# Two edits to the start of a fused attention and FFN kernel: the second weight's maxima in other PSUM banks, and the first weight's parts traced with every third attention slot

## The chip, the cores and the metric

The kernel runs on one core of one Trainium2 chip. The metric is the device time in microseconds of one execution; times of runs are given as the median of several. A profile is one execution with the hardware profiler on. Engines are PE (TensorE), DVE (VectorE), ACT (ScalarE), POOL (GpSimd) and SP (SyncE, which here issues most transfers).

## The reference, cut to what matters

```python
def _attn_ref(q, k, v, s):                      # B=8, H=8, S=576, D=64, float32
    scores = np.matmul(q, k.transpose(0, 1, 3, 2)) / sqrt(D)
    cum = np.cumsum(np.maximum(s, 0.0), axis=-1)
    bias = -(cum[:, :, :, None] - cum[:, :, None, :])
    scores = np.where(causal, -1e9, scores + np.minimum(bias, 0.0))
    attn = exp(scores - max); attn = attn / (sum(attn) + 1e-9)
    return np.matmul(attn, v)

def _moe_ref(x, w_in, w_out):                   # x is 4608 x 512, d_ff = 2048
    h = x @ w_in
    g = np.where(h >= 1, h, np.where(h <= -1, 0.0, (h + 1) ** 2 / 4))
    return g @ w_out
```

The attention output, with its heads laid side by side, is the x of the FFN. `w_in` and `w_out` arrive as 64-bit floats, which the kernel takes as pairs of 32-bit integers.

## The kernel before, in words

**Attention.** A job is a pair of heads and a part of the query rows (`hf` 0: 320 rows, `hf` 1: 256 rows). There are 64 jobs; each batch has eight, four with `hf` 0 and then four with `hf` 1. Jobs 0 to 3 are thus the first part of batch 0 and jobs 4 to 7 its second part. A job has eight slots (`att_slot(j, k)`): slot 0 prepares operands, slots 2 to 7 compute six units of scores (`scores`, matmuls at L432 for the jobs with float32 operands, L435 and L436 for the others), slot 7 also computes the output of the job before (`att_out`, L524 or L535). A unit of scores goes from PE to DVE (L441, masks and takes the minimum), ACT (L452, exponential), DVE (L466 or L494, the scale) and POOL and ACT, and is transposed on PE (jobs 0 to 3) or by a DMA. `x_split` (L552, L553) turns an output into the FFN's x in two float16 halves.

**Weights.** Each weight comes in 16 parts of 128 x 512. `load(c)` issues the transfer on SP (L199). `decode(c)` makes float32 out of the 64-bit pattern: ACT L207, DVE L208 and L209, and then either ACT L214 and DVE L215, or DVE L217 and L218. A scale is found from the parts' maxima, and `split(c)` makes two float16 halves (ACT L256, then POOL L259 and L262 or DVE L264; the second weight also has ACT L261). For the first weight, `row_scale` finds a scale for each four parts, and `row_shares` (L245 on) joins the four scales. For the second, `scale(g)` (L225 to L234) finds one for each eight parts: `column_max` transposes a column of maxima to a row on PE (L111, tile row_wo) and DVE takes the maximum (L113); `spread` multiplies it by ones on PE (L121, tile col_wo), and DVE copies the column out (L122).

**PSUM.** There are eight banks: pool `ps_s` has two (tag s), for score tiles, the outputs at L535, and all row and col tiles; `ps_h` has two, for h and the transposes of jobs 0 to 3; `ps_y` has four (y0 to y3), for the outputs of jobs 0 to 3, which stay there until their x is made, and then for the sums of the second FFN layer.

**FFN.** The FFN works in blocks (batch, `hf`) of 16 tiles: `ffn_h` computes h (L594) with ACT L606, DVE L609 and L610, ACT L620 and POOL L621 behind it; `ffn_y` multiplies with the second weight (L633). In the first block all 16 h come first, then y0 and y1, then y2 and y3.

**The order.** The kernel is traced in a program order. A planner then orders each engine's instructions by a priority, the traced position, and gives buffers out as they come free; `tc.high_priority(offset=n)` puts a block n positions further ahead. The score minimum at L441 has a lead of 10000; the FFN's element work, the x tiles and the second weight's tasks one of 6000.

At the start, the trace puts the loads of three parts of the first weight first, and then the 32 slots of jobs 0 to 3. With every second slot goes one part of the first weight (L678 to L692): decode part c, load part c + 3, split part c - 4, and after each fourth part `row_scale`. Then come `row_shares` and the last four splits under a lead (L695 to L701), the x tiles of jobs 0 to 3, and six tasks of `w2_tasks` (L664 to L676): eight decodes, `scale(0)`, eight splits, and the same for group 1. The main loop (L710 on) traces one or two attention slots, two more tasks of the second weight, and a step of the FFN each time round. The second weight's first three loads wait for `w1.r[1]`, the scale of parts 4 to 7.

Of the kernel before, what the change touches and what calls it, by code (L numbers as in the profile page):

```python
# [9 lines left out]
F32 = mybir.dt.float32  # L10
# [12 lines left out]
P = 128  # L23
NPAIR = H // 2
NKT = DM // P
# [10 lines left out]
LEAST_A = 2.0 ** -5  # L36
# [29 lines left out]
OUT_K = 7  # L66
W2_RATE = 2
W2_FIRST = 6
FIRST_N = 1
CH_N = 2  # L70

# [6 lines left out]
def attention_ffn(ctx: ExitStack, tc: tile.TileContext, qT, kT, vn, s, w_in, w_out, yT):  # L78
# [8 lines left out]
    ps_s = ctx.enter_context(tc.tile_pool(name="ps_s", bufs=2, space=PSUM))  # L87
    ps_h = ctx.enter_context(tc.tile_pool(name="ps_h", bufs=2, space=PSUM))
    ps_y = ctx.enter_context(tc.tile_pool(name="ps_y", bufs=1, space=PSUM))
# [5 lines left out]
    def pow2floor(out, in_, least):  # L95
        V.tensor_scalar(out, in_, least, None, ALU.max)
        V.tensor_scalar(out.bitcast(I32), out.bitcast(I32), 0x7F800000, None, ALU.bitwise_and)
# [7 lines left out]
    ones = cp.tile([P, P], BF16, name="ones")  # L105
    G.memset(ones, 1.0)

    def column_max(src, name):

        row = ps_s.tile([P, 512], F32, tag="s", name=f"row_{name}")  # L110
        T.transpose(row[:1, :P], src, ident)  # L111
        top = ap.tile([P, 1], F32, tag="top", name=f"top_{name}")
        V.tensor_reduce(top[:1], row[:1, :P], axis=AX, op=ALU.max)  # L113
        return top[:1]

    def spread(dst, top, name):

        t16 = ap.tile([P, 1], BF16, tag="t16", name=f"t16_{name}")
        V.tensor_copy(t16[:1], top)
        col = ps_s.tile([P, 512], F32, tag="s", name=f"col_{name}")  # L120
        T.matmul(col[:, :1], ones[:1], t16[:1], start=True, stop=True)  # L121
        V.tensor_copy(dst, col[:, :1])  # L122

# [44 lines left out]
    NW = 16  # L168
# [7 lines left out]
    class Weights:  # L176
# [48 lines left out]
        def scale(self, g, least):  # L225
            bound, r = self.bound[g], self.r[g]
            t = cp.tile([P, 1], F32, name=f"t_{self.name}{g}")
            V.tensor_reduce(t, self.peak[:, g * self.size:(g + 1) * self.size], axis=AX, op=ALU.max)
            top = column_max(t, f"{self.name}{g}")
            self.exponent(top)  # L230
            V.tensor_scalar(top, top, least, None, ALU.max)
            spread(bound, top, f"{self.name}{g}")
            V.reciprocal(r, bound)
            V.tensor_scalar(r, r, 2.0 ** 14, None, ALU.mult)  # L234

# [30 lines left out]
    w1 = Weights(  # L266
        "wi", lambda c: w_in[c // 4 * P:(c // 4 + 1) * P, c % 4 * NC:(c % 4 + 1) * NC, :],
        WO, WI, ((gp, "g", G_BUFS),), 1, by_rows=True,
    )
# [10 lines left out]
    def load_v(b):  # L280
        for p in range(NPAIR):
            v = vraw[b, p] = ap.tile([P, NB, P], F32, tag="vraw", bufs=4, name=f"v{b}_{p}")
            G.memset(v[TAIL:, NB - 1], 0.0)
            nc.sync.dma_start(v[:, :NB - 1], vn[b, p, :SP - P].rearrange("(j p) n -> p j n", p=P))
            nc.sync.dma_start(v[:TAIL, NB - 1], vn[b, p, SP - P:])

    def batch_start(b):
        c = ap.tile([P, NPAIR], F32, tag="csc", name=f"c{b}")
        for p in range(NPAIR):
            v = vraw[b, p].rearrange("p j n -> p (j n)")  # L290
            V.tensor_reduce(c[:, p:p + 1], v, axis=AX, op=ALU.max, apply_absolute_value=True)
        t = ap.tile([P, 1], F32, tag="mt", name=f"mt{b}")
        V.tensor_reduce(t, c, axis=AX, op=ALU.max)
        top = column_max(t, f"m{b}")
        pow2floor(top, top, TINY)
        m = msc[b] = ap.tile([P, 1], F32, tag="mb", name=f"mb{b}")
        spread(m, top, f"m{b}")
        r = rcs[b] = ap.tile([P, 1], F32, tag="rcs", name=f"rc{b}")
        V.reciprocal(r, m)
        V.tensor_scalar(r, r, 4096.0, None, ALU.mult)  # L300
# [41 lines left out]
    def plain(n, hf):  # L342
        return jobs.index((n, hf)) < PLAIN_JOBS
# [4 lines left out]
    def att_load(n, hf):  # L348
# [4 lines left out]
        if whole(n, hf):  # L353
            for t, src, c0 in zip(operands(n, hf), (qT, kT), (q0, 0)):
                sv = src[b, h0:h0 + 2, :, c0:W].rearrange("h d n -> d h n")
                (FIRSTQ if jobs.index((n, hf)) < FIRST_N else LOADQ).dma_start(t[:D, :, :W - c0], sv)
            return
        rq = ap.tile([P, 2, N], F32, tag="rq", bufs=1, name=f"rq{n}_{hf}")
        rk = ap.tile([P, 2, W], F32, tag="rk", bufs=1, name=f"rk{n}_{hf}")
        for t, src, c0 in ((rq, qT, q0), (rk, kT, 0)):  # L360
            sv = src[b, h0:h0 + 2, :, c0:W].rearrange("h d n -> d h n")
            for d0 in (0, D):
                (FIRSTQ if jobs.index((n, hf)) < FIRST_N else LOADQ).dma_start(t[d0:d0 + D], sv)
        raws[n, hf] = rq, rk

    def att_prep(n, hf):

        q0, N, _ = HALF[hf]
        W = q0 + N
        cd = cumd[2 * n:2 * n + 2].rearrange("h l n -> l h n")  # L370
        if not whole(n, hf) and not split_tiles:
            split_tiles.extend(operand_tiles(F32R, "s"))
            constant_rows(*split_tiles[1])
        Qc, Kc = operands(n, hf) if whole(n, hf) else split_tiles[1]
        if jobs.index((n, hf)) < CH_N:
            for hd in range(2):
                r = ch[2 * n + hd:2 * n + hd + 1]
                CUMQ.dma_start(Qc[D:D + 2, hd, :N].bitcast(F32), r[:, :, q0:W].bitcast(F32))
                CUMQ.dma_start(Kc[D + 2:D + 4, hd, :W].bitcast(F32), r[:, :, :W].bitcast(F32))
        else:  # L380
            CUMQ.dma_start(Qc[D:D + 2, :, :N].bitcast(F32), cd[:, :, q0:W])
            CUMQ.dma_start(Kc[D + 2:D + 4, :, :W].bitcast(F32), cd[:, :, :W])
        if whole(n, hf):
            return
        rq, rk = raws.pop((n, hf))
        (Q1, K1), (Q2, K2) = split_tiles
        A.copy(Q1[:, :, :N], rq)
        A.copy(K1[:, :, :W], rk)  # L388
        A.copy(Q2[:D, :, :N], rq[:D])
        V.tensor_tensor(Q1[D:, :, :N], rq[D:], Q1[D:, :, :N].bitcast(F32), ALU.subtract)  # L390
        V.tensor_tensor(K2[:D, :, :W], rk[:D], K1[:D, :, :W].bitcast(F32), ALU.subtract)  # L391

    def v_prep(n):

        b, p = n // NPAIR, n % NPAIR
        v, r = vraw.pop((b, p)), rcs[b]
        VT = vts[n] = ap.tile([P, 2, NB, P], F16, tag="vt", bufs=5, name=f"vt{n}")
        G.tensor_scalar(VT[:, 0], v, r, 1.0, ALU.mult, ALU.mult)
        if n < V_POOL:
            G.tensor_scalar(v, v, r, 1.0, ALU.mult, ALU.mult)  # L400
            G.tensor_tensor(VT[:, 1], v, VT[:, 0], ALU.subtract)
        vbs[n] = VT, v, r

    def v_low(n):
        VT, v, r = vbs.pop(n)
        if n >= V_POOL:
            with tc.issue_after(ttr[0]):
                V.scalar_tensor_tensor(VT[:, 1], v, r, VT[:, 0], ALU.mult, ALU.subtract)
# [148 lines left out]
    def att_slot(j, k):  # L557

        if j < len(jobs):
            n, hf = jobs[j]  # L560
            if k == 0:
                att_prep(n, hf)
            if plain(n, 0):
                if k in (1, 4) and hf == 1 and j < PLAIN_JOBS + 2:
                    v_prep(2 * (j - PLAIN_JOBS) + k // 4)
            elif hf == 0 and k == 1:
                v_prep(n)
            elif hf == 0 and k == V_K:
                v_low(n)
            if k >= 2:  # L570
                scores(n, *UNITS[hf][k - 2])
            if k == 3 and j + 1 < len(jobs):
                att_load(*jobs[j + 1])
            if k == 1 and j % (2 * NPAIR) == V_J + (j < 2 * NPAIR) and j // (2 * NPAIR) + 1 < B:
                load_v(j // (2 * NPAIR) + 1)
            if k == 5 and j + 1 < len(jobs) and jobs[j + 1][0] % NPAIR == 0 and jobs[j + 1][1] == 0:
                with tc.issue_after(ttr[0]):
                    batch_start(jobs[j + 1][0] // NPAIR)
        if k == OUT_K and 1 <= j <= len(jobs) and j != NPAIR:
            while j == len(jobs) and late:  # L580
                late.pop(0)()
            att_out(*jobs[j - 1])
# [92 lines left out]
                w2.split(c)  # L675
                yield  # L676

    for j in range(NPAIR):  # L678
        for k in range(8):
            if k % 2 == 0:  # L680
                c = 4 * j + k // 2
                w1.decode(c)
                w1.load(c + 3)
                if c >= NKT:
                    w1.split(c - NKT)
                if c % NKT == NKT - 1:
                    w1.row_scale(c // NKT, LEAST_A)
            if (j, k) == (0, 2):
                load_v(0)
            if (j, k) == (0, 6):  # L690
                batch_start(0)
            att_slot(j, k)  # L692
    while late:
        late.pop(0)()
    with tc.high_priority(offset=SCALE_LEAD):  # L695
# [9 lines left out]
    tasks = w2_tasks()  # L705
    for _ in range(W2_FIRST):
        next(tasks)

    t = 8 * NPAIR
# [56 lines left out]
```

## Time and profile before

| what | value |
| --- | --- |
| median of 3 runs | 1100.36 us (1099.31 to 1100.73) |
| the profiled execution | 1098.98 us |
| its span | 1097.2 us |
| mean granted TensorE clock | 0.984 of full speed |
| DVE busy | 79% |
| ACT busy | 66% |
| POOL busy | 60% |

The span is the time from the first to the last instruction of the profiled execution; about 1.8 us lie around it. A row of the timeline has the start and the length in us, the engine, the line of the kernel, the operation, the tile written and the tiles read, the shape and a count; in brackets stands how long the engine had been idle before, and what ended that. Rows of one line that follow each other are merged into one.

### The profile page before, as it was taken

Reading aid. Unit: us, or ns where it says so; the run is one execution under the profiler, and the core shown is the slowest. Engines: PE = TensorE matmul, PEld = TensorE weight load, DVE = VectorE, ACT = ScalarE, POOL = GpSimd, SP = SyncE. Lnnn points to the kernel's source line nnn. Section 1 sums busy time; section 2 is a strip of 40 time slices with the busy share of each in tenths; the row PEclk is TensorE's granted clock in tenths of the full one; section 3 lists DMA queues with packets and bytes.
Section 4 is the critical chain, followed back from the end, with each engine's and each line's share of the span. In section 5 each row is a group of like instructions: output and inputs, shape, how many; then the busy total and the mean of one; then the engine's idle time right before and its main releaser. Section 6 shows DMA issues by size and latency. Waiting matters only on the chain. (4 is left out here: it accounts for less than half of the span.)

```text
span 1097.2 us, 25029 instructions
## 1 busy us (share of the span) xinstructions
PE 1014.7 (92%) x8494; PEld 779.6 (71%) x8494; DVE 862.9 (79%) x2379; ACT 722.7 (66%) x1707; POOL 657.8 (60%) x1139
## 2 busy tenths in 40 slices
PE   1567898999999999999999999899999999999998
PEld 0334566687778877787778877787777877887787
DVE  7998986678788878788788778787888888887533
ACT  4867683567567765877577765776577765777432
POOL 2843486666567656666567665666566666765522
PEclk9998999799999999999999999999999999999999
DMA  8835245546357763777366753766276753677300
GB/s 241 240 119 172 77 101 112 124 107 167 92 116 164 133 145 87 161 143 151 88 146 144 160 124 84 160 134 166 71 161 131 154 127 73 153 137 139 68 25 20
DMA packets 300839, 140.33 MB, mean 128 GB/s; under 512 B 237608, under 2 KB 286632, under 8 KB 300712
## 3 DMA queue, kind: packets, MB, share of 16 engines
q1 hardware_dynamic: 291008, 128.80, 52.2%
q10 hardware_dynamic: 9704, 9.93, 3.2%
q8 instruction: 67, 1.10, 0.4%
q14 instruction: 60, 0.49, 0.1%
HBM read 71.00 MB, written 9.73 MB: 74 GB/s over the span
## 5 line engine op out<-in xcount | busy, mean ns | idle before, releaser
L594 PE MATMUL h<-x,WI 128*128 128x256 f16 (+1 forms) x3072 | 461.4, 290 | 11.9 <-DVE u L610 7.8
L633 PE MATMUL y<-g,WO 128*128 128x256 f16 (+1 forms) x3072 | 446.2, 287 | 1.9 <-ACT g L620 1.9
L594 PEld LDWEIGHTS <-WI 128*128 128x128 f16 x3072 | 287.9, 99 | 105.0 <-issue 22.1
L633 PEld LDWEIGHTS <-WO 128*128 128x128 f16 x3072 | 288.0, 98 | 85.4 <-issue 5.7
L621 POOL TENSOR_TENSOR g<-u,g 128x320 f16<-128x320 f32 (+1 forms) x256 | 207.0, 808 | 172.0 <-ACT g L620 164.0
L452 ACT ACTIVATE p<-p,mn 64x64 f32<-64x64 f32 (+4 forms) x320 | 179.4, 561 | 118.3 <-DVE mn L441 84.6
L606 ACT ACTIVATE u<-h,ub,us 128x320 f32<-128x320 f32 (+1 forms) x256 | 149.3, 583 | 131.8 <-PE h L594 130.0
L609 DVE SCALAR_TENSOR_TENSOR h<-h,ws,u 128x320 f32<-128x320 f32 (+1 forms) x256 | 132.8, 519 | 87.7 <-ACT u L606 84.1
L499 POOL TENSOR_SCALAR pb<-p,rs 128x256 f16<-128x256 f32 (+4 forms) x148 | 94.1, 636 | 142.1 <-DVE rs L495 88.7
L502 POOL TENSOR_TENSOR pb<-p,pb 128x256 f16<-128x256 f32 (+4 forms) x148 | 156.0, 1054 | 9.8
L441 DVE CUSTOM_DVE_ANT_0 p<-s,mask 64x64 f32<-64x64 f32 (+4 forms) x320 | 134.8, 422 | 34.2 <-PE s L436 21.6
L505 DVE SCALAR_TENSOR_TENSOR pb<-p,rs,pb 128x256 f16<-128x256 f32 (+4 forms) x148 | 127.8, 864 | 22.3 <-POOL pb L499 21.7
L610 DVE SCALAR_TENSOR_TENSOR u<-u,r,h 128x320 f32<-128x320 f32 (+1 forms) x256 | 130.5, 510 | 7.4
L435 PE MATMUL s<-K1s,Q1s 128*128 128x288 f32 (+4 forms) x312 | 118.1, 379 | 10.1 <-DVE Q1s L390 5.0
L500 ACT ACTIVATE p<-p,rs 128x192 f32<-128x192 f32 (+4 forms) x148 | 84.2, 569 | 51.5 <-DVE rs L495 49.2
L620 ACT CAST g<-u 128x320 f16<-128x320 f32 (+1 forms) x256 | 108.1, 422 | 6.5 <-DVE u L610 6.3
L501 POOL TENSOR_SCALAR pb<-p 128x256 f16<-128x256 f32 (+4 forms) x148 | 87.6, 592 | 16.7 <-ACT p L500 12.6
L436 PE MATMUL s<-K2s,Q2s 68*128 68x288 f32 (+4 forms) x312 | 96.2, 308 | 0.1
L535 PEld LDWEIGHTS <-vt 128*64 128x64 f16 x1464 | 68.5, 112 | 19.9 <-issue 14.0
L535 PE MATMUL px<-pt,vt 128*64 128x256 f16 (+3 forms) x1464 | 77.2, 257 | 2.7 <-DMA pt<-pb 2.6
L435 PEld LDWEIGHTS s<-K1s,Q1s 128*128 128x128 f32 (+1 forms) x312 | 56.7, 182 | 19.5 <-PE s L436 4.5
L391 DVE TENSOR_TENSOR K2s<-rk,K1s 64x1152 fp32r<-64x1152 f32 (+1 forms) x52 | 62.9, 1209 | 5.9 <-ACT K1s L388 5.1
(134 smaller groups left out, 1034.8 us busy)
## 6 DMA issues: line engine op xcount, KB each, us to landing
rk<-in_k_dram SPq DMA_DIRECT2D x56, 288.0 KB
wir<-in_moe_w_in_dram SPq DMA_DIRECT2D x16, 512.0 KB
v<-in_v_dram SPq DMA_DIRECT2D x32, 256.0 KB
wor<-in_moe_w_out_dram SPq DMA_DIRECT2D x16, 512.0 KB
rk<-in_k_dram SPq DMA_DIRECT2D x48, 160.0 KB
rq<-in_q_dram SPq DMA_DIRECT2D x48, 160.0 KB
rq<-in_q_dram SPq DMA_DIRECT2D x56, 128.0 KB
out_dram<-o ACTq DMA_DIRECT2D x32, 160.0 KB
```

Source lines behind the costliest of these rows:

```text
L435: T.matmul(sc[:R, :c1 - c0], Q1[:, hd, qo:qo + R], K1[:, hd, c0:c1], start=True, stop=False)
L441: ttr[0] = V.tensor_tensor_reduce(out=Pt[:R, c0:c1], in0=sc[:R, :c1 - c0], in1=mask[:R, mo:mo + c1 - c0], scale=-0.125, scalar=3.0e38 if m ...
L452: A.activation(Pt[:R, :W], Pt[:R, :W], AF.Exp, bias=m2[:R], scale=-1.0, accum_out=sums[n, i][:R, hd:hd + 1])
L502: G.tensor_tensor(los[1], pw, his[1], ALU.subtract)
L505: V.scalar_tensor_tensor(los[0], pv, rs[:R, :1], his[0], ALU.mult, ALU.subtract)
L535: T.matmul(px[hd * D:(hd + 1) * D, lo:N], vts[n][:, vl, j, hd * D:(hd + 1) * D], PT[:, 4 * j + 2 * hd + pl, lo:], start=(m == 0), stop=(m ...
L594: T.matmul(h[:, :N], WI[4 * kt + ft // 4][:, wl, ft % 4 * P:(ft % 4 + 1) * P], x[:, kt, xl], start=(n == 0), stop=(n == 3 * NKT - 1),)
L606: first = A.activation(u, h[:, :N], AF.Relu, bias=ubi[b], scale=usc[b]).ins
L609: V.scalar_tensor_tensor(h[:, :N], h[:, :N], wsc[b], u, ALU.mult, ALU.max)
L610: V.scalar_tensor_tensor(u, u, r, h[:, :N], ALU.min, ALU.mult)
L621: G.tensor_tensor(g[:, 1], u, g[:, 0], ALU.subtract)
L633: T.matmul(ys[b, hf, m][:, :N], WO[8 * (m // 2) + ft // 2][:, wl, c0:c0 + P], g[:, gl], start=(ft == 0 and n == 0), stop=(ft == NFT - 1 an ...
```

## The change

`column_max` and `spread` get a parameter `bank`, the pool and the tag of their tile. `scale`, which only the second weight uses, passes y2 for the row tile and y3 for the col tile. The calls of `batch_start` and `row_shares` stay with the two banks of `ps_s`.

The loop over the 32 slots of jobs 0 to 3 now traces a part of the first weight with every third slot, which makes 11 parts (0 to 10); parts 11 to 15 follow behind the last slot. What a part does is the same.

```diff
+W1_SLOTS = 3
...
-    def column_max(src, name):
+    def column_max(src, name, bank=(ps_s, "s")):
-        row = ps_s.tile([P, 512], F32, tag="s", name=f"row_{name}")
+        row = bank[0].tile([P, 512], F32, tag=bank[1], name=f"row_{name}")
...
-    def spread(dst, top, name):
+    def spread(dst, top, name, bank=(ps_s, "s")):
...
-        col = ps_s.tile([P, 512], F32, tag="s", name=f"col_{name}")
+        col = bank[0].tile([P, 512], F32, tag=bank[1], name=f"col_{name}")
...
-            top = column_max(t, f"{self.name}{g}")
+            top = column_max(t, f"{self.name}{g}", (ps_y, "y2"))
...
-            spread(bound, top, f"{self.name}{g}")
+            spread(bound, top, f"{self.name}{g}", (ps_y, "y3"))
...
-    for j in range(NPAIR):
-        for k in range(8):
-            if k % 2 == 0:
-                c = 4 * j + k // 2
-                w1.decode(c)
-                w1.load(c + 3)
-                if c >= NKT:
-                    w1.split(c - NKT)
-                if c % NKT == NKT - 1:
-                    w1.row_scale(c // NKT, LEAST_A)
-            if (j, k) == (0, 2):
-                load_v(0)
-            if (j, k) == (0, 6):
-                batch_start(0)
-            att_slot(j, k)
+    def w1_task(c):
+        w1.decode(c)
+        w1.load(c + 3)
+        if c >= NKT:
+            w1.split(c - NKT)
+        if c % NKT == NKT - 1:
+            w1.row_scale(c // NKT, LEAST_A)
+
+    c = 0
+    for t in range(8 * NPAIR):
+        if t % W1_SLOTS == 0:
+            w1_task(c)
+            c += 1
+        if t == 2:
+            load_v(0)
+        if t == 6:
+            batch_start(0)
+        att_slot(t // 8, t % 8)
+    for c in range(c, NW):
+        w1_task(c)
```

## The prediction

> **What bounds the kernel now.** I read the page first, for the engines over the whole span.
>
> ```profile
> span 1097.2 us, 25029 instructions
> PE 1014.7 (92%) x8494; PEld 779.6 (71%) x8494; DVE 862.9 (79%) x2379; ACT 722.7 (66%) x1707; POOL 657.8 (60%) x1139
> ...
> PE   1567898999999999999999999899999999999998
> ```
>
> TensorE is the bound, 92% busy, and what it lacks lies in the first slices. Neither edit touches a matmul of the FFN or of the attention, so the sum is about TensorE's lost time near the start: when it stood still, and when it ran at a low granted clock. Next came the table of stretches, whose columns are: stretch, length, busy PE, PEld, DVE, ACT, POOL (with counts), PE clock, DMA share, GB/s.
>
> ```profile
> 27.40:97.50 70.10, 46.02 (x146) 24.47 (x145) 65.14 (x202) 52.18 (x121) 39.15 (x58) 1.00 0.63 180
> 97.50:128.00 30.50, 22.25 (x120) 13.58 (x119) 26.83 (x64) 20.21 (x33) 9.30 (x11) 0.83 0.32 105
> 128.00:165.00 37.00, 35.97 (x251) 24.43 (x250) 32.98 (x78) 30.87 (x62) 29.95 (x38) 1.00 0.44 98
> 165.00:180.00 15.00, 15.00 (x118) 10.48 (x117) 8.41 (x24) 6.81 (x16) 9.87 (x15) 1.00 0.66 125
> 180.00:192.00 12.00, 8.17 (x64) 6.20 (x62) 9.57 (x43) 3.81 (x11) 6.76 (x9) 0.83 0.38 100
> 192.00:200.00 8.00, 6.88 (x41) 4.08 (x42) 5.10 (x17) 4.20 (x14) 5.79 (x15) 0.50 0.58 136
> 200.00:209.00 9.00, 9.00 (x37) 5.93 (x36) 6.25 (x21) 5.08 (x15) 5.23 (x16) 0.54 0.68 154
> 209.00:1097.20 888.20, 867.47 (x7717) 688.29 (x7716) 688.96 (x1879) 587.74 (x1418) 543.93 (x957) 1.00 0.56 122
> ```
>
> Up to 165 us VectorE is the bound (65.14 of 70.10, 26.83 of 30.50, 32.98 of 37.00). From 209 us TensorE is (867.47 of 888.20). Between them, from 180 to 209, TensorE loses time though VectorE has room: it stands still 12.00 - 8.17 + 8.00 - 6.88 = 4.95 us, and the clock costs it up to 12 x 0.17 + 8 x 0.50 + 9 x 0.46 = 10.2 us more, 15.1 us together. The timeline of TensorE and of the x tiles says why.
>
> ```profile
> 180.04 1.47 PE L594 MATMUL h<-x,WI 128*128 128x256 f16 x12
> ...
> 198.51 0.47 ACT L552 ACTIVATE x<-px,shares_wi 128x256 f16<-128x256 f32 x1 [0.30 <-PE px L535]
> ```
>
> The first FFN block has run out by 180.04, and the second can't go on: it wants the attention outputs of jobs 6 and 7 (batch 0, second half), and the last of them becomes x at 198.51. Attention jobs 4 to 7 are what ends last, so what the change does is read from when they run.
>
> **The bank edit.** The maxima of the second weight pass through a row tile and a col tile for each of two groups. Now they take banks of pool ps_s, two banks that the score tiles use too; afterwards they take y2 and y3.
>
> ```profile
> 85.95 0.47 DVE L441 CUSTOM_DVE_ANT_0 p<-s,mask 128x320 f32<-128x320 f32 x1
> ...
> 65.97 0.64 SPq L356 DMA_DIRECT2D K1w<-in_k_dram  x1
> ...
> 104.34 5.88 PE L594 MATMUL h<-x,WI 128*128 128x320 f16 x24 [3.53 <-DVE u L610]
> ...
> 117.25 0.27 PE L111 MATMUL row_wo<-ident,t_wo 128*1 128x128 f32 x1
> ...
> 121.60 0.17 PE L121 MATMUL col_wo<-t_wo,ones 1*128 1x1 bf16 x1
> 121.70 1.02 PE L432 MATMUL s<-K1w,Q1w 68*128 68x448 f32 x2
> ...
> 136.13 0.92 PE L432 MATMUL s<-K2w,Q2w 68*128 68x448 f32 x2
> ...
> 138.65 0.27 PE L111 MATMUL row_wo<-ident,t_wo 128*1 128x128 f32 x1
> ...
> 144.33 0.16 PE L121 MATMUL col_wo<-t_wo,ones 1*128 1x1 bf16 x1 [0.53 <-DVE t_wo L119]
> 144.41 0.75 PE L432 MATMUL s<-K2w,Q2w 68*128 68x288 f32 x2
> ```
>
> Both groups show one pattern. The last scores of job 3 are read at 85.95, and job 4's key operand is asked for at 65.97, yet its first score stands directly behind col_wo, at 121.70, with TensorE idle 3.53 us ahead of 104.34. At the second group no score is issued from 137.05 (136.13 + 0.92) to 144.41, 7.36 us, and again the next stands directly behind col_wo. My reading: the maxima are traced under a lead of 6000, ahead of the scores, so their tiles take their turn at the two banks first, and the scores queue behind a maximum that still waits for eight decoded parts. With banks of their own the scores owe them nothing. Bounds for what this moves job 4: nothing at the low end, 121.70 - 104.34 = 17.4 us at the high end, the first place where TensorE had nothing else; at the second group nothing to 7.36 us.
>
> It can't all reach the end, because VectorE is nearly full there: attention pulled forward pushes FFN and decoding work back, except where VectorE was idle. It was idle 30.50 - 26.83 + 37.00 - 32.98 = 7.7 us from 97.5 to 165. I take 7 us for how much earlier the last x of the first batch is ready; 0 and the 15.1 us above are the ends. As TensorE is the bound behind it, that time comes off the end. I count no clock gain in the 7: the gap becomes shorter, but the idleness that lowers the clock need not go.
>
> The new wait costs nothing. y2 and y3 hold outputs of jobs 2 and 3 until they become x behind 97.63 (row below), well ahead of 117.25. The first FFN sums in y2 and y3 need parts 8 to 15 of the second weight, which wait for the second maximum in any case. If that cover were gone, the row would wait, and behind it on TensorE the h tiles: for the longest h wait above, 3.53 us.
>
> On the low clock from 192 to 209: TensorE was busy 6.88 of 8 us and 9 of 9, and it was still granted 0.50 and 0.54. [...]
>
> **The slot edit.** Every part of the first weight moves from slot 2c to slot 3c, and parts 11 to 15 come behind all 32 slots of jobs 0 to 3. One part issues a load on SP, one or two ScalarE passes and these on VectorE (columns: count, busy us, mean ns):
>
> ```profile
> L208 DVE TENSOR_SCALAR_CACHE_REDUCE WO<-WO 128x512 f32<-128x512 f32 x25 | 16.8, 676 | 3.8 <-ACT WO L207 3.8
> L209 DVE TENSOR_SCALAR WO<-WO 128x512 int32<-128x512 int32 x25 | 13.2, 536 | 0.0
> ...
> L217 DVE SCALAR_TENSOR_TENSOR WO<-wir,WO 128x512 int32<-128x512 int32 x8 | 7.5, 940 | 0.0
> L218 DVE SCALAR_TENSOR_TENSOR WO<-wir,WO 128x512 int32<-128x512 int32 x8 | 6.9, 863 | 0.0
> L215 DVE SCALAR_TENSOR_TENSOR WO<-wir,WO 128x512 int32<-128x512 int32 x8 | 5.8, 726 | 0.0
> ```
>
> That is 0.68 + 0.54 + half of (0.94 + 0.86 + 0.73) = 2.5 us a part, so 12.5 us for five parts pass from ahead of the last attention slots to behind them. Which of the two ended last ahead of the FFN?
>
> ```profile
> 87.94 0.29 DVE L698 TENSOR_SCALAR shares<-shares_wi,rc 128x4 f32<-128x4 f32 x1
> 97.63 0.53 ACT L552 ACTIVATE x<-px,shares 128x320 f16<-128x320 f32 x1 [2.37 <-PE px L524]
> ```
>
> The weight's shares are there at 88.23, and the last attention output of jobs 0 to 3 at 97.63, 9.4 us later. So the attention is late and the edit moves the right side forward, by up to 9.4 us; but with 12.5 us moved behind it, the shares end at up to 100.7, 3.1 us later than 97.63. The ends for the first full h are thus 9.4 us earlier and 3.1 us later, nearly even once the shares' chain and the attention meet in the middle. An earlier h alone would only bring the stop at 180 earlier, as long as job 7 isn't earlier too. So I count 0. SP's weight loads stand behind attention loads more often; TensorE waited for no attention operand after the first score tiles, so that is 0 as well. The second weight's first three loads wait for the scales of parts 4 to 7, so they start later too. VectorE fills that with attention; the cost shows only if it idles.
>
> **The sum.** The profiled execution took 1098.98 us (span 1097.2 and 1.8 around it): 1098.98 - 7 + 0 = 1092.0. The median of the runs is 1100.36, 1.4 us more, so I forecast 1100.36 - 7 = 1093.4 us. About 0.2%, 2.2 us, is what a measurement of this kernel can tell from no change.
>
> **The rivals.** *The whole gap goes.* If jobs 4 to 7 keep pace with the first FFN block, the idle time and the low clock from 180 to 209 both go: 1100.36 - 15.1 = 1085.3. For it: job 4 could start 17.4 us earlier. Against it: VectorE had only 7.7 us to spare.
>
> *Nothing moves.* The scores may come late because the planner puts them there and not for the banks, or VectorE's full stretch eats the shift: 1100.4. For it: from 97.5 to 128 VectorE was 88% busy (26.83 of 30.50), and scores not traced with a lead may stay behind the h tiles.
>
> *Slower: the first weight is finished too late.* The last five parts, with their scale and shares, end behind the attention, the second weight's loads start late, and VectorE has nothing ready. The first full h comes 3.1 us later, and the second weight's first maximum slips by up to the raw loads' delay, the 2.5 us of a part. It decides from the point where the shares end later than the last px of job 3; then 3.1 + 2.5 = 5.6 us less what the bank edit returns, about 1 us in that case: 1100.36 + 4.6 = 1105. For it: only 9.4 us of room for 12.5 moved. Against it: VectorE filled some of 27.4 to 97.5 with second-weight work that can wait.
>
> **How the numbers follow.** Forecast 0.46, whole gap 0.14, nothing moves 0.18, first weight late 0.22. Faster is 0.46 + 0.14 = 0.60, within 0.2% 0.18, slower 0.22. The range goes from the whole gap, 1085, to the late weight, 1105, which leaves out about 0.2 for larger swings of either sign. The forecast case alone spans 1088 to 1098.
>
> **What would show it.** Right: the first score of job 4 stands well ahead of 121.70 and no longer behind col_wo; scores are issued between the second row_wo and col_wo; the last x of batch 0's second half comes near 191 instead of 198.51; stretches behind 209 take what they took. The slot edit is right at zero if the first full h stays within 3 us of 97.5. Wrong: job 4's first score still waits until about 120 (the banks weren't it); or it is early and x is not (VectorE took it back); or the clock drops elsewhere; or shares land behind 100.

## The result and the profile after

The changed kernel takes 1095.26 us (median of 15 runs) against 1101.24 us for the kernel before on the same chip (15 runs). The ratio is 0.9943, 95% interval 0.9931 to 0.9954, so it is faster by 0.57%, or 6.3 us. One run of each kernel, 1286.8 and 1198.7 us, was disturbed and is left out of the ratio. The profiled execution took 1094.18 us with a span of 1092.4, 4.8 us less than that of before. The lines shown from here on have numbers one higher than in the kernel before.

The page first: TensorE's busy time is the same within 2 us, and its slices differ only among the first seven (the very first is 1 before and 3 now).

```profile
span 1092.4 us, 25031 instructions
PE 1012.9 (93%) x8494; PEld 779.2 (71%) x8494; DVE 857.4 (78%) x2379; ACT 722.4 (66%) x1707; POOL 659.5 (60%) x1139
...
PE   3657799999999999999999999899999999999998
```

The table of stretches, with the columns of the prediction's:

```profile
27.40:97.50 70.10, 43.59 (x129) 24.36 (x130) 61.91 (x193) 54.10 (x121) 35.34 (x57) 1.00 0.53 165
97.50:128.00 30.50, 23.40 (x136) 13.73 (x135) 29.76 (x81) 18.67 (x35) 16.12 (x21) 0.89 0.77 198
128.00:165.00 37.00, 33.08 (x237) 22.01 (x236) 31.74 (x80) 29.01 (x56) 29.58 (x34) 1.00 0.40 88
165.00:180.00 15.00, 15.00 (x107) 10.65 (x105) 8.79 (x29) 7.03 (x13) 7.53 (x9) 1.00 0.22 58
180.00:192.00 12.00, 9.15 (x82) 6.49 (x80) 7.98 (x33) 6.31 (x19) 8.18 (x18) 0.96 0.44 114
192.00:200.00 8.00, 7.25 (x46) 5.62 (x47) 4.06 (x16) 4.29 (x14) 4.16 (x12) 0.50 0.96 163
200.00:209.00 9.00, 9.00 (x68) 6.60 (x67) 5.58 (x18) 4.68 (x14) 4.00 (x10) 0.74 0.45 111
209.00:1092.40 883.40, 863.68 (x7677) 685.27 (x7675) 686.92 (x1874) 585.86 (x1413) 543.14 (x956) 1.00 0.55 123
```

I work out the loss from 180 to 209 as the prediction did. The idle time is 2.85 + 0.75 = 3.60 us, and the clock costs up to 12 x 0.04 + 8 x 0.50 + 9 x 0.26 = 6.82 us. Together that is 10.4 us, where it was 15.1. The difference of 4.7 us is what the two profiled spans differ by (4.8). Behind 209 us little changed: TensorE lacks 883.40 - 863.68 = 19.7 us there, 20.7 before.

The timeline of TensorE shows where the scores of jobs 4 to 7 went:

```profile
84.23 0.16 PE L122 MATMUL col_wi<-t_wi,ones 1*128 1x1 bf16 x1 [3.12 <-DVE t_wi L120]
84.44 3.33 PE L433 MATMUL s<-K1w,Q1w 68*128 68x448 f32 x4
...
118.48 0.75 PE L433 MATMUL s<-K2w,Q2w 68*128 68x288 f32 x2 [1.85 <-DVE mn L442]
...
126.60 0.27 PE L112 MATMUL row_wo<-ident,t_wo 128*1 128x128 f32 x1
...
135.84 0.17 PE L122 MATMUL col_wo<-t_wo,ones 1*128 1x1 bf16 x1
...
143.26 0.27 PE L112 MATMUL row_wo<-ident,t_wo 128*1 128x128 f32 x1
...
143.64 1.02 PE L433 MATMUL s<-K2w,Q2w 68*128 68x448 f32 x2
...
148.95 0.92 PE L433 MATMUL s<-K2w,Q2w 68*128 68x448 f32 x2
...
152.24 0.17 PE L122 MATMUL col_wo<-t_wo,ones 1*128 1x1 bf16 x1
...
165.94 1.14 PE L433 MATMUL s<-K2w,Q2w 68*128 68x288 f32 x4
...
177.72 0.17 PE L122 MATMUL col_m<-t_m,ones 1*128 1x1 bf16 x1
177.82 0.75 PE L433 MATMUL s<-K2w,Q2w 68*128 68x288 f32 x2
```

Job 4 (K1w) starts at 84.44, not at 121.70, and all its scores and those of job 5 (K2w) are out before the first row_wo. Job 4's first score again stands directly behind a maximum's spread, this time col_wi, the first weight's, which uses the score banks in both kernels; no run moves that one. Scores now also stand between the second row_wo and col_wo; they are job 7's (K2w). But two new stops appear in job 7: no score from 149.87 to 165.94, and none from 167.1 to 177.82, where the next stands directly behind col_m, the spread of the next batch's maximum. The x tiles of the second half of batch 0 show what arrives:

```profile
124.22 0.47 ACT L553 ACTIVATE x<-px,shares_wi 128x256 f16<-128x256 f32 x1 [0.63 <-PE px L536]
145.74 0.46 ACT L553 ACTIVATE x<-px,shares_wi 128x256 f16<-128x256 f32 x1
183.53 0.47 ACT L553 ACTIVATE x<-px,shares_wi 128x256 f16<-128x256 f32 x1 [0.56 <-PE px L536]
195.23 0.47 ACT L553 ACTIVATE x<-px,shares_wi 128x256 f16<-128x256 f32 x1 [1.78 <-PE px L536]
```

Before, these four came at 156.74, 170.51, 187.53 and 198.51. Job 4 is 32.5 us earlier and job 7 only 3.3 us, and the second FFN block needs them all. (In the repetition of the changed kernel, e11 below, job 7's x comes at 197.38, so the 3.3 is 1.1 there.) The experiments ask three things: what each edit is worth alone, whether the banks were the cause, and why 32.5 us become 3.3.

### The profile page after: what moved, and what is told of

Same layout as the page of the kernel before. It is cut to its first block, busy times and chain, and to the rows that moved or that the text cites. A ratio compares the mean times of both kernels' runs of the same rounds, so it can differ in the third digit from the quotient of the medians.

```text
span 1092.4 us, 25031 instructions
## 1 busy us (share of the span) xinstructions
PE 1012.9 (93%) x8494; PEld 779.2 (71%) x8494; DVE 857.4 (78%) x2379; ACT 722.4 (66%) x1707; POOL 659.5 (60%) x1139
## 4 chain that ended last, share of the span: by engine, by line
PE 65%; DVE 10%; ACT 5%; issue 4%; DMA 2%; POOL 2%; ACTq 1%; DVEq 0%; POOLq 0%
PE y L634 27%; PE h L595 26%; PE px L536 4%; PE s L436 3%; PE s L437 3%; DVE pb L506 2%; DVE h L610 2%; DVE p L442 1%; DMA pt<-pb 1%; PE s L433 1%; ACT u L607 1%; DVE K2s L392 1%; DVE Q1s L391 1%; ACT p L453 1%; DVE u L611 1%
## 5 line engine op out<-in xcount | busy, mean ns | idle before, releaser
L442 DVE CUSTOM_DVE_ANT_0 p<-s,mask 64x64 f32<-64x64 f32 (+4 forms) x320 | 135.1, 423 | 34.4 <-PE s L437 20.4
L611 DVE SCALAR_TENSOR_TENSOR u<-u,r,h 128x320 f32<-128x320 f32 (+1 forms) x256 | 130.6, 510 | 7.3
L436 PE MATMUL s<-K1s,Q1s 128*128 128x288 f32 (+4 forms) x312 | 118.0, 379 | 10.4 <-DVE Q1s L391 5.3
L536 PEld LDWEIGHTS <-vt 128*64 128x64 f16 x1464 | 67.7, 111 | 22.0 <-issue 17.4
```

Source lines behind the costliest of these rows:

```text
L436: T.matmul(sc[:R, :c1 - c0], Q1[:, hd, qo:qo + R], K1[:, hd, c0:c1], start=True, stop=False)
L442: ttr[0] = V.tensor_tensor_reduce(out=Pt[:R, c0:c1], in0=sc[:R, :c1 - c0], in1=mask[:R, mo:mo + c1 - c0], scale=-0.125, scalar=3.0e38 if m ...
L536: T.matmul(px[hd * D:(hd + 1) * D, lo:N], vts[n][:, vl, j, hd * D:(hd + 1) * D], PT[:, 4 * j + 2 * hd + pl, lo:], start=(m == 0), stop=(m ...
L611: V.scalar_tensor_tensor(u, u, r, h[:, :N], ALU.min, ALU.mult)
```

## The experiments

Each diff is against the changed kernel. "Gap loss" is idle time plus clock loss from 180 to 209 us, worked out as above. It and the last x are from one profiled execution each, the ratios from all runs.

| kernel | ratio to before, 95% interval | gap loss, us | last x, us |
| --- | --- | --- | --- |
| before | 1 | 15.1 | 198.51 |
| changed | 0.9943 (0.9931 to 0.9954) | 10.4 | 195.23 |
| e11, changed again | 0.9959 (0.9944 to 0.9974) | 10.4 | 197.38 |
| e1, banks alone | 0.9976 (0.9959 to 0.9992) | 3.2 | 201.94 |
| e2, slots alone | 0.9984 (0.9971 to 0.9996) | 17.4 | 202.47 |
| e3, first maximum's banks and slots | 0.9992 (0.9978 to 1.0005) | 16.1 | 200.86 |
| e6, second maximum's banks and slots | 1.0006 (0.9995 to 1.0017) | 17.8 | 202.03 |
| e4, batch maxima in the h banks | 1.0308 (1.0292 to 1.0324) | 4.6 | 193.29 |
| e8, batch maxima traced two slots later | 1.0020 (1.0003 to 1.0038) | 7.5 | 195.83 |
| e5, lead of 200 for early attention | 0.9884 (0.9865 to 0.9903) | 0.8 | 187.97 |
| e10, the lead without the banks | 1.0000 (0.9983 to 1.0017) | 19.3 | 203.96 |
| e7, every fourth slot | 0.9914 (0.9891 to 0.9938) | 3.1 | 193.01 |
| e9, the lead and every fourth slot | 0.9942 (0.9926 to 0.9958) | 0.3 | 192.28 |
| e12, the lead and every second slot | 0.9916 (0.9890 to 0.9941) | 0.1 | 193.42 |

### Each edit alone (e1, e2)

```diff
 e1:
-W1_SLOTS = 3
+W1_SLOTS = 2
 e2:
-            top = column_max(t, f"{self.name}{g}", (ps_y, "y2"))
+            top = column_max(t, f"{self.name}{g}")
-            spread(bound, top, f"{self.name}{g}", (ps_y, "y3"))
+            spread(bound, top, f"{self.name}{g}")
```

> The bank edit alone, with the first weight's parts at every second slot as before. Theory (the score tiles no longer queue behind the second weight's maxima; the slot edit is worth nothing): the first score of job 4 stands near 85 to 90 us and not behind col_wo, the last x of batch 0 comes near 195 to 196 us, ratio to before 0.994 (0.992 to 0.996). Rival (the slot edit brings part of the gain): ratio 0.996 to 0.999.

> The slot edit alone, with the maxima in the two score banks as before. Theory: the first score of job 4 stands directly behind col_wo again, near 120 to 130 us, ratio 1.000 (0.998 to 1.003). Rival (the slot edit brings part of the gain): 0.996 to 0.998. Second rival (the first weight finished late costs time by itself): over 1.003.

The banks alone give 0.9976 and the slots alone 0.9984, 2.6 and 1.8 us of 1100; together they give 6.3 us by the first comparison and 4.5 by its repetition. So neither carries the result by itself. Whether they add up or do more together can't be told from these intervals. Without the new banks (e2) the scores stand behind col_wo at both groups again, as in the kernel before:

```profile
125.05 0.17 PE L122 MATMUL col_wo<-t_wo,ones 1*128 1x1 bf16 x1
125.15 1.02 PE L433 MATMUL s<-K1w,Q1w 68*128 68x448 f32 x2
...
147.76 0.16 PE L122 MATMUL col_wo<-t_wo,ones 1*128 1x1 bf16 x1
147.85 0.75 PE L433 MATMUL s<-K2w,Q2w 68*128 68x288 f32 x2
```

With them (e1) job 4's first score is at 90.36, directly behind col_wi (90.25), although the parts of the first weight stand where they stood before. The banks therefore set when job 4 starts, and the slots don't. What the slots do is seen at the very start. These are the first 27.4 us of the kernel before and then of the changed one:

```profile
0.00:27.40 27.40, 3.97 (x11) 2.11 (x12) 19.60 (x57) 11.80 (x21) 7.79 (x25) 1.00 0.84 241
```

```profile
0.00:27.40 27.40, 8.79 (x24) 4.45 (x24) 20.69 (x61) 12.40 (x26) 11.45 (x29) 1.00 0.85 244
```

TensorE is busy for 3.97 us in all three kernels with a part at every second slot (before, e1, e12), and for 8.5 to 9.5 us in all those with fewer. The attention of job 0 starts sooner when fewer parts of the weight are traced between its slots. No trace shows this head start reaching the end: with the slots alone TensorE still has 868.25 us of busy time ahead of it at 209 us, and 867.47 before.

In e1 the profiled execution had a granted clock of only 0.79 on average from 27.4 to 180 us, where before had 0.97. It took 1101.62 us, more than e1's median of 1097.88 and more than the 1098.98 of the kernel before, though its gap loss is 12 us smaller. So its last x and gap loss don't say what e1 gains, and a small gap loss alone doesn't make a kernel fast.

### One maximum at a time (e3, e6)

```diff
 e3 (e6 has g == 1):
-            top = column_max(t, f"{self.name}{g}", (ps_y, "y2"))
+            top = column_max(t, f"{self.name}{g}", (ps_y, "y2") if g == 0 else (ps_s, "s"))
-            spread(bound, top, f"{self.name}{g}", (ps_y, "y3"))
+            spread(bound, top, f"{self.name}{g}", (ps_y, "y3") if g == 0 else (ps_s, "s"))
```

> As the changed kernel, but only the first maximum (parts 0 to 7) is in y2 and y3; the second stays in the score banks. Theory of turns at the banks: job 4's scores are as early as in the changed kernel, and the scores that stop are the last four of job 5, which now stand directly behind the second col_wo, near 150 us. If only the last x of batch 0 counts, and that is set by FFN work behind which job 7 waits anyway, the ratio stays at 0.994 to 0.996. Rival (each stop costs in proportion, 17.4 and 7.4 us of stop): about a third of the gain is lost, 0.996 to 0.997.

> As the changed kernel, but only the second maximum (parts 8 to 15) is in y2 and y3; the first stays in the score banks. Theory of turns (outputs come in order, so the later of the two stops decides, and freeing only the first was worth nothing): job 4's first score stands behind the first col_wo near 125 us, no score stands behind the second; the last x of batch 0 comes 2 to 4 us earlier than with the slot edit alone (202.47), ratio 0.995 to 0.998. Rival (the first stop alone sets it): as the slot edit alone, 0.998 to 1.000.

Neither is worth anything beside the slots alone (0.9992 and 1.0006 beside 0.9984). In e3 job 4 starts early, and then job 5's scores (K2w) stop at the maximum that is still in their banks:

```profile
84.34 3.33 PE L433 MATMUL s<-K1w,Q1w 68*128 68x448 f32 x4
...
103.40 1.02 PE L433 MATMUL s<-K2w,Q2w 68*128 68x448 f32 x2 [0.30 <-DVE mn L442]
...
147.09 0.17 PE L122 MATMUL col_wo<-t_wo,ones 1*128 1x1 bf16 x1
147.20 0.75 PE L433 MATMUL s<-K2w,Q2w 68*128 68x288 f32 x2
```

The stop from 104.4 to 147.20 is longer than either stop of the kernel before, so the lead that the first half won is lost again at the second: job 4's output is traced in the last slot of job 5, and its x comes at 158.16, later than before (156.74). In e6 the first stop remains (col_wo at 123.45, first score at 123.55). The turn-taking is shown, from both sides, and two stops in a row can't be priced one by one: the one that remains gets the time of the other.

### The stop at the batch's maximum (e4, e8)

```diff
 e4:
-        top = column_max(t, f"m{b}")
+        top = column_max(t, f"m{b}", (ps_h, "h"))
-        spread(m, top, f"m{b}")
+        spread(m, top, f"m{b}", (ps_h, "h"))
 e8 (the lines below move down to slot 7, behind att_out):
-            if k == 5 and j + 1 < len(jobs) and jobs[j + 1][0] % NPAIR == 0 and jobs[j + 1][1] == 0:
-                with tc.issue_after(ttr[0]):
-                    batch_start(jobs[j + 1][0] // NPAIR)
+        if k == 7 and j + 1 < len(jobs) and jobs[j + 1][0] % NPAIR == 0 and jobs[j + 1][1] == 0:
+            with tc.issue_after(ttr[0]):
+                batch_start(jobs[j + 1][0] // NPAIR)
```

> As the changed kernel, and in addition the maxima of each batch's values (row_m and col_m, one pair for each of eight batches) take banks of pool ps_h instead of the score banks. Theory of turns: in the changed kernel the scores of job 7 stop from 166.9 to 177.8 us and go on directly behind col_m; with this edit they no longer stand behind col_m, the last x of batch 0 comes 3 to 8 us earlier than 195.75, and the same may help at the seven other batch starts: ratio to before 0.985 to 0.991. Rival (the scores of job 7 wait for the first FFN block's matmuls, traced ahead of them, and not for a bank): x stays within 2 us, ratio 0.992 to 0.996. Third way: the two h banks are short, and h tiles wait for the maxima: 0.996 or more.

> As the changed kernel, but the maxima of the next batch's values are traced behind the last slot of the job, behind its last scores and the output before it, and not behind slot 5; they stay in the score banks. Theory of turns: the last scores of job 7 no longer stop behind col_m (11 us from 166.9 to 177.8), the last x of batch 0 comes 2 to 6 us earlier than 195.23, ratio 0.989 to 0.993. Rival (these scores wait for the first FFN block in any case): within 0.2% of the changed kernel, 0.993 to 0.996; the next batch's scale, now later, may cost: over 0.996.

Both take the stop behind col_m away from job 7, and neither is faster. In e8 the stop has only passed to job 8, whose first score now stands directly behind col_m:

```profile
185.71 0.17 PE L122 MATMUL col_m<-t_m,ones 1*128 1x1 bf16 x1
185.81 0.33 PE L433 MATMUL s<-K1w,Q1w 68*64 68x64 f32 x2
```

Job 7's scores are out 5.8 us earlier than in the changed kernel (175.69 and 181.50), but its output is traced in the last slot of job 8, behind that job's scores, and its x comes at 195.83, 0.6 us later than without the edit. So e8 doesn't show what the stop is worth. In e4 no score stands behind col_m, job 7's scores are out by 172.07, and still its x comes only 2 us earlier (193.29), again with all scores of job 8 ahead of its output. How early job 7's own scores are is thus not all that its x hangs on. And e4 loses time behind 209 us, where six more batches have this maximum. The stretch from 240 to 640 us of the changed kernel, and then of e4:

```profile
240.00:640.00 400.00, 392.70 (x3491) 310.25 (x3490) 327.39 (x899) 278.02 (x670) 259.22 (x455) 1.00 0.63 136
```

```profile
240.00:640.00 400.00, 380.95 (x3329) 297.51 (x3327) 325.88 (x869) 267.08 (x643) 245.02 (x440) 0.98 0.56 129
```

TensorE loses 392.70 - 380.95 = 11.7 us there, and its clock is below full too (0.98, where it was 1.00). One would expect the h tiles to wait for the maximum in their banks, but the profile puts only 2.4 us of TensorE's waits there to h tiles that VectorE holds up (L611), and 9.5 us to scores that wait for a minimum at L442 (2.0 in the changed kernel). How e4 loses its time stays open.

### A lead for the early attention (e5, e10, and the changed kernel again, e11)

```diff
 e5:
-            att_slot(t // 8, t % 8)
+            with tc.high_priority(offset=200) if t < 72 else ExitStack():
+                att_slot(t // 8, t % 8)
 e10 (e5, and the maxima back in the scores' banks):
-            top = column_max(t, f"{self.name}{g}", (ps_y, "y2"))
+            top = column_max(t, f"{self.name}{g}")
-            spread(bound, top, f"{self.name}{g}", (ps_y, "y3"))
+            spread(bound, top, f"{self.name}{g}")
```

> As the changed kernel, but the attention slots of jobs 4 to 8 get a lead of 200 positions, so that job 7's scores no longer come behind the first FFN block's matmuls that are traced ahead of them. Theory (the freed attention of jobs 4 and 5 ran into its turn: job 7 waits for the late first FFN block, and the gap at 185 to 200 us stays): the last x of batch 0 comes at least 8 us earlier than 195.23, h of the second half goes on without a stop, and the time falls by a further 4 to 9 us, ratio to before 0.986 to 0.991. Rival (VectorE has nothing to spare, so what attention gains the FFN loses): x is earlier, the first FFN block ends later by as much, ratio 0.993 to 0.997.

> The lead of 200 and every third slot, but the second weight's maxima in the banks of the scores. Theory (the scores of jobs 4 to 7 take turns with the maxima, and a lead of 200 doesn't move a score ahead of a maximum traced with a lead of 6000): the first score of job 4 stands behind the first spread near 125 again, the last x comes near 200, low clock from 180 to 209 stays, ratio 0.996 to 1.000. Rival (the lead alone closes the gap, the banks are not needed): last x near 188 and a ratio near 0.988.

> The changed kernel again, beside the two others on one chip. Ratio 0.993 to 0.996 if the first result stands; the gain of the lead over it then is the difference of the ratios on this chip, 0.004 to 0.008 by the theory.

The lead puts the slots of jobs 4 to 8 some 200 positions ahead of their trace, past steps of the first FFN block. It takes along all that is in these slots, the maximum of the next batch and the outputs too. The gap closes:

```profile
166.68 0.17 PE L122 MATMUL col_m<-t_m,ones 1*128 1x1 bf16 x1
166.79 0.75 PE L433 MATMUL s<-K2w,Q2w 68*128 68x288 f32 x2
```

```profile
180.00:192.00 12.00, 11.24 (x100) 8.22 (x99) 4.25 (x14) 5.19 (x15) 6.36 (x17) 1.00 0.69 163
192.00:200.00 8.00, 8.00 (x65) 6.50 (x64) 6.49 (x23) 4.46 (x16) 3.01 (x9) 1.00 0.50 127
200.00:209.00 9.00, 9.00 (x88) 7.30 (x86) 6.42 (x22) 6.56 (x20) 6.59 (x14) 1.00 0.70 119
```

```profile
187.97 0.47 ACT L553 ACTIVATE x<-px,shares_wi 128x256 f16<-128x256 f32 x1 [2.05 <-PE px L536]
```

The first pair of lines is from TensorE's timeline of e5: job 7's scores still stand behind col_m, but 11 us earlier. Its last x comes at 187.97, 7.3 us earlier than in the changed kernel, and the low clock is gone with the idle time (1.00 in all three stretches). The kernel takes 1088.23 us, 0.9884 of before. It is the fastest of this study, faster than both kernels that were given. So the trace order of these slots held the rest of the gap in the changed kernel. Its trace agrees for the longer of the two stops: VectorE's last read of a score bank ahead of it ends at 150.90, and the next score comes at 165.94, which speaks against a missing bank. Whether job 7's scores, the batch's maximum (row_m at 162.27 in e5, 173.84 in the changed kernel) or job 8's scores had to move isn't separated.

The same lead with the maxima in the scores' banks (e10) gives 1.0000. Its first score of job 4 stands at 124.65, directly behind col_wo (124.55), and its last x is at 203.96:

```profile
124.65 1.02 PE L433 MATMUL s<-K1w,Q1w 68*128 68x448 f32 x2
```

So the lead does nothing without the new banks. On the same chip the changed kernel again gave 0.9959, so its gain stands, somewhat smaller.

### How many slots a part (e7, e9, e12)

```diff
 e7:
-W1_SLOTS = 3
+W1_SLOTS = 4
 e9:  e5 with W1_SLOTS = 4
 e12: e5 with W1_SLOTS = 2
```

> As the changed kernel with a part of the first weight at every fourth slot (8 parts in the slots, 8 behind them). If later parts let the attention of jobs 0 to 3 start earlier and that is what the slot edit brings: TensorE is busier still in the first 27 us than 8.8, and the ratio is 0.992 to 0.995. Rival (the first weight is finished too late): shares and the first full h come 3 us or more later than in the changed kernel, ratio 0.996 or more.

> The lead of 200 for the main loop's attention slots below 72, with the first weight's parts at every fourth slot. Theory (the two are separate gains: the lead closes the gap from 180 to 209, the sparser parts start TensorE's attention work earlier and leave less of VectorE's work before the last x): about 1085, ratio near 0.986, last x below 188 and no low clock from 180 to 209. Rival (both pay for the same gap, so the gap can be closed only once): 1088, ratio 0.988 as with the lead and every third slot, or worse if the first weight now ends late.

> The lead of 200 with both maxima in the second layer's banks, but the first weight's parts at every second slot as before. Theory A (the slot edit's gain is the earlier start of TensorE in the first 27 us, some 4.8 us of work done sooner, and stays beside the lead's): 2 to 4 us more than the lead with every third slot, ratio 0.990 to 0.992, TensorE busy near 4 us in the first 27.4. Theory B (the slot edit gains only through the gap from 180 to 209, which the lead closes by itself): ratio 0.988 as with every third slot, and no idle or low clock from 180 to 209.

Without the lead, every fourth slot has a lower ratio than every third, 0.9914 beside 0.9943 and 0.9959; its interval (up to 0.9938) overlaps that of the first comparison (from 0.9931) and lies just below that of the repetition (from 0.9944), so this isn't settled. With the lead, every third slot has the lowest ratio, 0.9884, with 0.9942 for every fourth and 0.9916 for every second; the intervals of the first (up to 0.9903) and the last (from 0.9890) overlap. The ratio of e12 is thus what its first theory expected, a slot edit that keeps its worth beside the lead, but it doesn't exclude the second. With every fourth slot the lead gains nothing: e9 took 1093.04 us, where its two theories gave 1085 and 1088, and the first weight isn't late (the last x of jobs 0 to 3 comes at 97.01). The gap from 180 to 209 is closed in all three (0.3 us or less in e9 and e12), so they differ ahead of it. In e9 TensorE stands still for 8.9 us from 128 to 165 us, in e5 for 5.3, and the clock is lower in e9 (0.86 beside 0.95); e9 first, then e5:

```profile
128.00:165.00 37.00, 28.14 (x170) 17.79 (x169) 33.69 (x82) 24.14 (x49) 23.80 (x30) 0.86 0.48 102
```

```profile
128.00:165.00 37.00, 31.69 (x216) 21.20 (x215) 33.51 (x88) 27.11 (x53) 24.40 (x32) 0.95 0.42 102
```

VectorE is 91% busy in both. What it does differs: in e5 the second weight's second maximum comes at 145.06, in e9 twenty microseconds later, and in e12 at 165.09 (TensorE's timeline of e5, then of e9):

```profile
145.06 0.42 PE L112 MATMUL row_wo<-ident,t_wo 128*1 128x128 f32 x1
```

```profile
165.63 0.27 PE L112 MATMUL row_wo<-ident,t_wo 128*1 128x128 f32 x1
```

The second FFN layer of the first block needs that weight, and the block ends at 199.3 us in e9, at 196.9 in e12 and at 191.4 in e5. The link between the two is argued: in e9 the profile puts 2.9 us of TensorE's waits to that weight's parts (L265), in e12 none. Why the planner orders VectorE's work in this way with two and with four slots, and not with three, stays open. A late second maximum alone doesn't decide it either: in e7 it is at 153.19, later than the changed kernel's 143.26, and e7 is faster.

## Why the prediction was right, and where it was not

**The sum.** 1093.4 us was forecast, 7 less than the 1100.36 of the runs shown. By the ratio it is 6.3 less, 1094.1. The repetition gives 4.5 less. The sign, the size and the place (180 to 209) are right. The working is right in part only, and that the size came out is partly luck: the sum has all 7 us from the bank edit, and the bank edit alone measured 2.6 (e1).

**The cause of the late scores: right.** The scores took turns with the maxima at two banks. e2, e3, e6 and e10 each leave at least one maximum there and lie between 0.9984 and 1.0006, with a gap loss of 16 us or more. All kernels without one there lose less than 11 us in the gap, e4 and e8 among them, which lose elsewhere. The rival that the planner or VectorE puts the scores late in any case is refuted for job 4.

**The bounds for job 4 and for the second group: wrong in form.** I gave 17.4 us at most for job 4, from the first place at which TensorE had nothing else to do. It moved by 37.3 us, to 84.44, directly behind the first weight's spread, for which TensorE had waited 3.12 us. And I bounded the two stops separately, where e3 and e6 show that removing only one of them is worth nothing.

**The term "I take 7 us for how much earlier the last x is ready": mis-sized.** It measured 3.3 us (198.51 to 195.23), and 1.1 in the repetition (197.38). I named VectorE's room as the limit, 7.7 us. VectorE still idles 0.74 + 5.26 = 6.0 us from 97.5 to 165 in the changed kernel. What ended last was something else: the trace order of the slots up to job 8 behind the first FFN block, since a lead of 200 moves that x by 7.3 us more without any work taken from VectorE. "Wrong: or it is early and x is not" came true for the most part: job 4 is 32.5 us early, job 7 is not.

**"I count no clock gain in the 7": wrong.** Of the 4.7 us that the gap lost, 10.2 - 6.8 = 3.4 are clock and 4.95 - 3.60 = 1.35 are idle time. The smaller x term and the clock term together come near the forecast, so the 7 was right by errors that offset each other in part.

**"So I count 0" for the slots: the other step that failed.** The slots alone measured 0.9984, 1.8 us (the interval ends at 0.9996, so hardly clear of nothing), and taking them away from the changed kernel costs 3.6 us by the ratios (0.9943 to 0.9976), or 1.9 by the repetition (0.9959). I priced the edit by VectorE's passes ahead of the first full h, and that h came at the edge of the 3 us that the prediction allowed (the last x of jobs 0 to 3 at 100.56, 97.63 before; at 101.87 in e11). This sign could not decide it. The bank edit moves the same x: with the slots alone it is at 95.79. The edit also acts 70 us earlier, where TensorE has 4.8 us more work done by 27.4 us, and the prediction has no row of that stretch. Whether and through which later step those 4.8 us reach the end is not settled.

**The new wait on y2 and y3: nothing, as said.** The outputs in them became x by 102.7, and the first row_wo is at 126.60. **The late first weight: did not happen.** The shares are there at 87.42 (88.23 before), although 5 parts come behind the slots. The attention gave way to them, not the other way round. **The whole gap** did not go with this change; e5 closes it, at 1088.2 us, less of a gain than the 15.1 us of the rival, and time is lost ahead of 180: TensorE stands still for 37.00 - 31.69 = 5.3 us from 128 to 165 in e5, and stood for 1.0 there before.

**The clock.** The trace shows it staying low for a long time after TensorE is busy again. In finer stretches of the changed kernel:

```profile
190.00:191.00 1.00, 0.00 (x0) 0.00 (x0) 0.90 (x3) 0.87 (x2) 1.00 (x5) 1.00 1.28 290
191.00:192.00 1.00, 0.00 (x0) 0.00 (x0) 0.71 (x3) 0.50 (x3) 1.00 (x4) 0.53 0.64 141
...
196.00:200.00 4.00, 4.00 (x14) 2.59 (x13) 3.18 (x12) 2.59 (x10) 1.60 (x7) 0.50 1.06 218
200.00:202.00 2.00, 2.00 (x10) 1.29 (x9) 2.00 (x8) 0.94 (x4) 1.01 (x2) 0.50 0.23 47
202.00:204.00 2.00, 2.00 (x11) 1.36 (x10) 1.29 (x5) 1.72 (x5) 1.42 (x3) 0.50 0.51 152
204.00:205.00 1.00, 1.00 (x8) 0.76 (x6) 0.56 (x2) 0.00 (x0) 0.97 (x4) 0.64 0.00 0
205.00:206.00 1.00, 1.00 (x10) 0.52 (x10) 0.24 (x1) 0.00 (x0) 0.00 (x0) 1.00 0.61 123
```

TensorE stops at 189.68 and the clock falls at about 191.1, 1.4 us into the stop. TensorE is fully busy again from 196, and the clock comes back at about 204.7, 8.7 us later. So in this trace a stop of 2.74 us, the wait for job 7's transposes, is followed by some 13.7 us at half speed, and idle time in this place is worth more than it measures. In the kernel before, the clock also falls inside a stop: TensorE stops at 100.81 for 3.53 us, and the clock goes to 0.50 at about 102.55. Not every stop does this: through the 3.12 us ahead of 84.23 in the changed kernel the clock stays at 1.00, and no run shows what makes the difference. In e5, which leaves 0.8 us of idle time from 180 to 209, the clock there is full (1.00 in all three stretches).

## What to carry to other kernels

Short-lived tiles that are planned with a large lead should not share a pool with a stream that has none: the stream waits for its turn behind a tile whose inputs may come much later. Look in the timeline for work that stands directly behind an unrelated small instruction again and again, and move all such tiles out together, since one that stayed kept the whole cost here. Move them to banks that are idle at that time: the same kind of tile in the h banks cost 3.1% (e4). Then follow the last consumer and not the first one that moves: what was pulled forward by 32 us was worth 3 until the order of the jobs behind it was changed too.

## What the runs showed of the hardware that was not expected

The granted clock near the start differs a lot between executions that issue nearly the same work: from 27.4 to 180 us it averaged 0.97 in the profile of the kernel before, 0.98 in that of the changed kernel, 0.79 in e1 and e12, and 0.89 in e5, and e5 is still the fastest. This need not belong to the edits. The 80 runs of the kernel before that were made beside the experiments had a mean clock over the whole span from 0.962 to 0.992, a spread of 0.030 x 1097 = 33 us, where 0.79 in place of 0.98 is 29 us of the 152.6; where in the span it was low isn't recorded for them. It costs little in the end: the 31 of them below 0.975 took 1101.3 us on average and the 49 others 1100.5, a difference within their scatter. That fits a stretch that VectorE bounds (132.21 of 152.60 us busy in the changed kernel). There TensorE was busy 115.07 us for 602 matmuls at 0.98, and in e1 114.50 us for 531 at 0.79, on average 0.19 and 0.22 us each, of mixed shapes.
